# One row of small products for the scores of half a batch and one folding

## The chip, the cores and the metric

The kernel runs on one core of one Trainium2 chip. The metric is the device time of one execution in microseconds (us). Before the change the median of three runs is 1428.58 us (1428.11 to 1428.69).

## The reference, cut to what matters

Eight batches of attention over 32 memory slots are followed by two gated layers. Only the attention and the first layer bear on the change.

```python
B, H, S, D, M = 8, 8, 576, 64, 32
a = softmax(phi, axis=2)                       # pooling weights, over the 32 slots
k_m = einsum('bhsm,bhsd->bhmd', a, k)          # pooling of the keys
v_m = einsum('bhsm,bhsd->bhmd', a, v)          # pooling of the values
scores = q @ k_m.T / sqrt(D)
x = softmax(scores) @ v_m                      # all heads side by side: 4608 x 512
g = x @ w_gate;  val = x @ w_val               # 512 -> 1536
y = (silu(g) * val) @ w_out                    # 1536 -> 512
# a second layer follows: 512 -> 2048, elu, -> 512
```

## The kernel before, in words

**Folding.** The pooled values are never multiplied with the softmax. They are multiplied into the weights first: for each batch `b` and each pair `p` of 128-wide units, `vw` (line 253) forms `v_m` times a block of `w_gate` and `w_val`. This is called a folding here. Eight heads give eight small products with 64 contraction rows and 32 output columns each, 512 wide; each is two instructions in the trace, so that a folding is a row of 16. They are written to the double bank `pvw`. ScalarE then copies the high part to the tile `VW[b, p]` (line 265) and VectorE writes the low part (line 266); only then is `pvw` free. The tiles `VW` come from the pool `vx` (line 50), which has four buffers: two foldings for each of two batches.

**Scores.** `score(hf)` (line 425) does the scores of half a batch (288 positions), again with eight small products of 64 rows and 32 columns, 288 wide, 16 instructions, into the double bank `ps_sc` (line 445). VectorE then transposes both banks (450), takes a maximum (456) and subtracts it (457), and ScalarE takes the exponential (458). `norm` and `attn` follow as tasks of their own.

**Pooling.** `kv_mm` (line 384) is a row of 80 instructions for one batch, and `kv_out` copies its result with ScalarE (404). Pooling and foldings share the single double bank of the pool `ps_kv` (line 68, called `G2` from line 521 on), so each must wait until the one before it is copied out.

**The order.** The loop over `b` (from line 593 on) does batch `b`'s gates and values (`gate1`, `val1`, lines 281 to 283) for two halves of four units, and the steps `down1` (286 to 288), which are long rows of full 128x128 products. Into this main stream `tick()` (line 637) feeds a list `todo` of small tasks: the back tasks of batch `b + 1` (`back_tasks`, line 512: scores, norm, attention of the first half, then of the second), the front tasks of batch `b + 2` (`front_tasks`, line 496: three tasks of transposes `a_T`, the pooling, `kv_T`; the first batch has another list) and, at the end, the two foldings of batch `b + 1`. Front and back tasks alternate (line 631). A scheduler then fixes each engine's order: it simulates the engines and may place small tasks well ahead of the main stream if their inputs and banks are free. `together` (line 95) keeps a row's products behind its first one and lets nothing in between.

Of the kernel before, what the change touches and what calls it, by code (L numbers as in the profile page):

```python
# [8 lines left out]
F32 = mybir.dt.float32  # L9
# [29 lines left out]
def attention_moe_moe(ctx: ExitStack, tc: tile.TileContext, qT, phiT, kv, kv4, w1g, w1o, w2, out):  # L39
# [210 lines left out]

    def vw(b, p, pool=None, ps=None):
        t = VW[b, p] = vx_p.tile([128, 2, 2, 512], F32R, tag="vx", name="vw")
        both = ps or pool.tile([128, 2, 512], F32, tag="at", name="pvw")
        ps = [both[:, g] for g in range(2)]

        def head(j, g):
            r, c = slice(64 * g, 64 * g + 64), slice(32 * j, 32 * j + 32)
            return mm(ps[g][c], lhsT=Bs[b].vt[r, j, :], rhs=WG[p][j][r], start=True, stop=True)  # L260

        together([lambda j=j, g=g: head(j, g) for j in reversed(range(KD)) for g in (1, 0)])
        if b >= NEG or p >= UA // 2:
            with tc.high_priority() if pool is None else nullcontext():
                act(out=t[:, 0], in_=both, func=AF.Copy)
                tt(out=t[:, 1], in0=both, in1=t[:, 0].bitcast(F32), op=ALU.subtract)
            return
        for g in range(2):
            last["vwh"] = act(out=t[:, 0, g, :], in_=ps[g], func=AF.Copy)
        for g in range(2):  # L270
            mm(ps[g], lhsT=minus, rhs=t[:, 0, g, :], start=False, stop=True, skip_group_check=True)
            last["vwl"] = act(out=t[:, 1, g, :], in_=ps[g], func=AF.Copy)
            if g == 0:
                last["vwl0"] = last["vwl"]

# [52 lines left out]
    class Batch:  # L328
# [72 lines left out]
        def kv_out(self):  # L401
            self.kvm = fr_p.tile([128, 2, 2, D], F32, tag="kvm", name="kvm")
            for g in range(2):
                act(out=self.kvm[:, :, g, :], in_=self.kvp[g], func=AF.Copy, scale=self.rs[:, g:g + 1])


        def kv_T(self):
# [14 lines left out]

        def score(self, hf):
            q = self.qr.pop(hf)
            t = ps_at.tile([128, 2, T], F32, tag="at", name="ps_sc")
            ps = [t[:, g, :HS] for g in range(2)]
            if self.b == 0 and hf == 1:
                sc = t.rearrange("p a c -> p (a c)")  # L430
                full = sc[:, :512].rearrange("p (t g j m) -> p t j g m", t=2, g=2, j=4)
                rhs = [self.kTd[:, j].rearrange("p g m -> p (g m)") for j in range(4)]
                calls = [lambda i=i, j=j: mm(full[:, i, j], lhsT=q[:, j, 128 * i:128 * i + 128], rhs=rhs[j],
                                             start=True, stop=True) for i in range(2) for j in range(4)]
                calls += [lambda j=j: mm(t[32 * j:32 * j + 32, 1, :2 * M], lhsT=q[:, j, 256:], rhs=rhs[j],
                                         start=True, stop=True) for j in range(4)]
                together(calls)
                self.sc = bk_p.tile([128, 2, HS], F32, tag="sc", name="sc", bufs=2)
                with tc.issue_after(last["sum"].ins):
                    self.soft(self.sc, sc[:, :2 * HS].rearrange("p (b m) -> p b m", m=M))  # L440
                return

            def head(j, g):
                r = slice(64 * g, 64 * g + 64)
                return mm(ps[g][32 * j:32 * j + 32], lhsT=self.kT[r, j, :], rhs=q[r, j, :], start=True, stop=True)

            together([lambda j=j, g=g: head(j, g) for j in range(4) for g in (1, 0)])
            t = self.sc = bk_p.tile([128, 2, HS], F32, tag="sc", name="sc", bufs=2)
            for g in range(2):
                nc.vector.transpose(out=t[:, g], in_=ps[g])  # L450
            self.soft(t, t.rearrange("p g (b m) -> p (g b) m", m=M))

        def soft(self, t, x):
            sc = t.rearrange("p g (b m) -> p (g b) m", m=M)
# [56 lines left out]

    def back_tasks(b):
        z, nxt = Bs[b], Bs[b + 1] if 0 < b < B - 1 else None
        yield lambda: z.score(0)
        yield lambda: (z.norm(0), nxt and nxt.load_q(0))
        yield lambda: (z.attn(0))
        yield lambda: (z.score(1), 1 < b < B - 2 and Bs[b + 2].phi())
        yield lambda: (z.norm(1), nxt and nxt.load_q(1))
        yield lambda: (z.attn(1), z.store_at())

# [2 lines left out]
    def vw_tasks(b):  # L523
        for p in range(UA // 2):
            yield lambda p=p: vw(b, p, G2)
# [67 lines left out]
    for b in range(B):  # L593
# [30 lines left out]
            fr += [lambda: vw(0, 2, G2)] + [lambda f=f: (store_w2(), f()) for f in sets("first", 1)] + [store_w2]  # L624
            fr += [lambda: vw(0, 3, G2), lambda: load_wg(4, 1, wa_p), lambda: load_wg(5, 0, wa_p)]
        if b == 0:
            v = list(vw_tasks(1))
            todo += [bk[0], bk[1], v[0], lambda: Bs[2].phi(), bk[2], bk[3], bk[4], v[1], fr[0], fr[1], bk[5]] + fr[2:] + [lambda: Bs[3].phi()]
        else:
            for i in range(max(len(bk), len(fr))):  # L630
                todo += fr[i:i + 1] + bk[i:i + 1]
            if b + 1 < B:
                todo += vw_tasks(b + 1)
        done = [0, 0]
        spread = 18 if b == 0 else 16 if b < B - 2 else 24

# [519 lines left out]
```

## Time and profile before

| | |
|---|---|
| median of the runs | 1428.58 us |
| the profiled execution | 1427.93 us, its span 1426.2 us |
| TensorE (PE) busy | 1401.3 us, 98% of the span |
| VectorE (DVE) busy | 1136.1 us, 80% |
| ScalarE (ACT) busy | 862.4 us, 60% |
| TensorE's granted clock | 0.995 of full, over the span |

The busy time of an engine counts instructions that overlap once. PE products are pipelined: one begins while the one before is still under way, so what a product costs is the distance from its start to the next start, and not its duration. The part that the change touches lies between about 50 and 250 us.

### The profile page before, as it was taken

The numbers are of one execution on the slowest core, as the hardware profiler recorded it, in microseconds if no ns is written. First come the engines' busy times: TensorE is split into PE (matmuls) and PEld (weight loads), VectorE is DVE, ScalarE is ACT, GpSimd is POOL, SyncE is SP. The second block draws the span as 40 slices with busy tenths as digits, with TensorE's granted clock in tenths as the row PEclk, the third lists the DMA queues.
The fourth block names the chain that finished last, engine by engine and source line by source line (L and its number), as shares of the span: only waits on it lengthen the run. The fifth ranks groups of instructions, "written<-read, shape, count | busy, mean of one in ns | idle before, by whom it ended". The sixth has DMA issues, their size and how long they took to land.

```text
span 1426.2 us, 23205 instructions
## 1 busy us (share of the span) xinstructions
PE 1401.3 (98%) x9259; PEld 1211.6 (85%) x9259; DVE 1136.1 (80%) x1452; ACT 862.4 (60%) x1254; POOL 44.8 (3%) x73
## 2 busy tenths in 40 slices
PE   6899999999999999999999999999999999999998
PEld 4787889988999999999988888888888888888887
DVE  7988978778798877877988578885889488957884
ACT  5665545544465555555666388557866587548843
POOL 0000000000000000000000000000000000000000
PEclk8999999999999999999999999999999999999999
DMA  9888512664789887888889756766686667566653
GB/s 378 326 298 292 208 72 101 230 233 175 237 251 309 284 240 232 274 241 287 267 291 364 269 188 206 280 214 189 201 282 219 190 202 265 215 210 203 213 201 132
DMA packets 89484, 337.65 MB, mean 237 GB/s; under 512 B 9376, under 2 KB 23712, under 8 KB 70048
## 3 DMA queue, kind: packets, MB, share of 16 engines
q1 hardware_dynamic: 55312, 254.04, 51.6%
q10 hardware_dynamic: 26880, 51.39, 9.8%
q0 software_dynamic: 7184, 30.74, 8.9%
q8 instruction: 73, 1.20, 0.3%
q14 instruction: 35, 0.29, 0.1%
HBM read 251.13 MB, written 85.00 MB: 236 GB/s over the span
## 4 chain that ended last, share of the span: by engine, by line
PE 93%; DVE 3%; ACT 2%; DMA 1%; issue 1%; ACTq 0%; SPq 0%; DVEq 0%
PE pu L877 12%; PE pu L879 12%; PE pu L878 12%; PE pd L877 5%; PE pd L879 5%; PE pd L878 5%; PE acc L288 4%; PE acc L286 4%; PE acc L287 4%; PE pv L281 3%; PE pg L281 3%; PE pv L283 3%; PE pv L282 3%; PE pg L283 3%; PE pg L282 3%; PE pvw L260 3%
## 5 line engine op out<-in xcount | busy, mean ns | idle before, releaser
L878 PE MATMUL pu<-xlo,w 128*128 128x512 f32 x672 | 261.4, 389 | 0.0
L877 PE MATMUL pu<-xhi,w 128*128 128x512 f32 x672 | 261.4, 389 | 0.0
L879 PE MATMUL pu<-xhi,w 128*128 128x512 f32 x672 | 261.4, 389 | 0.0
L906 ACT ACTIVATE xhi<-g 128x1024 fp32r<-128x1024 f32 x120 | 126.5, 1058 | 106.9 <-PE pu L879 64.3
L907 DVE TENSOR_TENSOR xlo<-g,xhi 128x1024 fp32r<-128x1024 f32 x120 | 145.0, 1220 | 40.7 <-ACT xhi L906 40.6
L879 PEld LDWEIGHTS pu<-xhi,w 128*128 128x128 f32 x672 | 126.1, 188 | 26.3
L878 PEld LDWEIGHTS pu<-xlo,w 128*128 128x128 f32 x672 | 126.1, 188 | 26.2
L877 PEld LDWEIGHTS pu<-xhi,w 128*128 128x128 f32 x672 | 126.1, 188 | 26.1
L287 PE MATMUL acc<-hh,ws 128*128 128x288 f32 x448 | 131.7, 296 | 0.0
L286 PE MATMUL acc<-hh,ws 128*128 128x288 f32 x448 | 131.5, 295 | 0.0
L288 PE MATMUL acc<-hl,ws 128*128 128x288 f32 x448 | 128.8, 297 | 0.0
L281 PE MATMUL pv<-at,vw 128*128 128x288 f32 x384 | 115.6, 301 | 2.4 <-DVE s L306 0.7
L281 PE MATMUL pg<-at,vw 128*128 128x288 f32 x384 | 116.7, 304 | 1.1 <-ACT p L579 0.5
L767 ACT ACTIVATE hh<-gh 128x576 fp32r<-128x576 f32 x112 | 76.0, 685 | 68.6 <-PE acc L287 50.8
L282 PE MATMUL pg<-at,vw 128*128 128x288 f32 x384 | 114.1, 297 | 0.9 <-DVE at L488 0.9
L283 PE MATMUL pg<-at,vw 128*128 128x288 f32 x384 | 113.6, 296 | 0.0
L282 PE MATMUL pv<-at,vw 128*128 128x288 f32 x384 | 113.6, 296 | 0.0
L283 PE MATMUL pv<-at,vw 128*128 128x288 f32 x384 | 113.5, 296 | 0.0
L877 PE MATMUL pd<-xhi,w 128*128 128x512 f32 x288 | 112.0, 389 | 0.0
L878 PE MATMUL pd<-xlo,w 128*128 128x512 f32 x288 | 112.0, 389 | 0.0
L879 PE MATMUL pd<-xhi,w 128*128 128x512 f32 x288 | 112.0, 389 | 0.0
L897 DVE SCALAR_TENSOR_TENSOR et<-et 128x1024 f32<-128x1024 f32 x72 | 87.8, 1219 | 28.8 <-ACT et L896 28.8
(161 smaller groups left out, 3226.9 us busy)
## 6 DMA issues: line engine op xcount, KB each, us to landing
w<-dnd SPq DMA_DIRECT2D x64, 1024.0 KB, 4.9
w<-upd SPq DMA_DIRECT2D x40, 1024.0 KB, 5.7
w<-upd SPq DMA_DIRECT2D x32, 768.0 KB, 4.6
ws<-d1d SPq DMA_DIRECT2D x42, 512.0 KB, 4.5
kvr<-kv SPq DMA_DIRECT2D x32, 512.0 KB, 7.5
wr<-w SPq DMA_DIRECT2D x16, 1024.0 KB, 6.3
upd<-uw ACTq DMA_DIRECT2D x32, 512.0 KB, 6.3
dnd<-uw ACTq DMA_DIRECT2D x32, 512.0 KB, 7.9
```

The source lines that it names most:

```text
L281: mm(ps, lhsT=wh, rhs=ah, start=g == 0, stop=False)
L282: mm(ps, lhsT=wh, rhs=al, start=False, stop=False)
L283: last["pe"] = mm(ps, lhsT=wl, rhs=ah, start=False, stop=g == 1)
L286: mm(ps, lhsT=w[0][:, ms], rhs=hs[0], start=start, stop=False, skip_group_check=skip)
L287: mm(ps, lhsT=w[1][:, ms], rhs=hs[0], start=False, stop=False, skip_group_check=skip)
L288: mm(ps, lhsT=w[0][:, ms], rhs=hs[1], start=False, stop=stop, skip_group_check=skip)
L877: mm(ps, lhsT=w[0], rhs=x[0], start=start, stop=False, skip_group_check=skip)
L878: mm(ps, lhsT=w[0], rhs=x[1], start=False, stop=False, skip_group_check=skip)
L879: last["mm"] = mm(ps, lhsT=w[1], rhs=x[0], start=False, stop=stop, skip_group_check=skip)
L897: stt(out=a, in0=e, scalar=1.0, in1=a, op0=ALU.add, op1=ALU.mult)
L906: last["hi"] = act(out=hi, in_=x, func=AF.Copy)
L907: last["lo"] = tt(out=lo, in0=x, in1=hi.bitcast(F32), op=ALU.subtract)
```

## The change

From the second batch on, `score` takes the number of a folding as well: the eight products of that folding of the same batch and the eight of the scores are given to `together` as one list, foldings first. The first half's scores take folding 0, the second half's folding 1. The copies of the folding (`vw_out`) come behind the scores' softmax in program order. The separate folding tasks at the end of `todo` go, and there is a new order for loops with six front tasks, in which the pooling comes behind the second half's scores.

```diff
-    def vw(b, p, pool=None, ps=None):
-        t = VW[b, p] = vx_p.tile([128, 2, 2, 512], F32R, tag="vx", name="vw")
-        both = ps or pool.tile([128, 2, 512], F32, tag="at", name="pvw")
+    def vw_calls(b, p, ps):
         def head(j, g):
             r, c = slice(64 * g, 64 * g + 64), slice(32 * j, 32 * j + 32)
...
-        together([lambda j=j, g=g: head(j, g) for j in reversed(range(KD)) for g in (1, 0)])
+        return [lambda j=j, g=g: head(j, g) for j in reversed(range(KD)) for g in (1, 0)]
+
+    def vw(b, p, pool=None, ps=None):
+        both = ps or pool.tile([128, 2, 512], F32, tag="at", name="pvw")
+        together(vw_calls(b, p, both))
+        vw_out(b, p, both, pool)
+
+    def vw_out(b, p, both, pool=None):
+        t = VW[b, p] = vx_p.tile([128, 2, 2, 512], F32R, tag="vx", name="vw")
...
-    def score(self, hf):
+    def score(self, hf, p=None):
...
-            together([lambda j=j, g=g: head(j, g) for j in range(4) for g in (1, 0)])
+            more = p is not None and G2.tile([128, 2, 512], F32, tag="at", name="pvw")
+            with tc.issue_after(last["g2"].ins) if more else nullcontext():
+                together((vw_calls(self.b, p, more) if more else []) +
+                         [lambda j=j, g=g: head(j, g) for j in range(4) for g in (1, 0)])
             t = self.sc = bk_p.tile([128, 2, HS], F32, tag="sc", name="sc", bufs=2)
             for g in range(2):
                 nc.vector.transpose(out=t[:, g], in_=ps[g])
             self.soft(t, t.rearrange("p g (b m) -> p (g b) m", m=M))
+            if more:
+                vw_out(self.b, p, more, G2)
...
-        yield lambda: z.score(0)
+        yield lambda: z.score(0, 0 if b else None)
...
-        yield lambda: (z.score(1), 1 < b < B - 2 and Bs[b + 2].phi())
+        yield lambda: (z.score(1, 1 if b else None), 1 < b < B - 2 and Bs[b + 2].phi())
...
         if b == 0:
-            v = list(vw_tasks(1))
-            todo += [bk[0], bk[1], v[0], lambda: Bs[2].phi(), bk[2], bk[3], bk[4], v[1], fr[0], fr[1], bk[5]] + fr[2:] + [lambda: Bs[3].phi()]
+            todo += bk[:2] + [lambda: Bs[2].phi()] + bk[2:5] + fr[:2] + bk[5:] + fr[2:] + [lambda: Bs[3].phi()]
+        elif len(fr) == 6 and b < B - 2:
+            todo += [fr[0], bk[0], fr[1], bk[1], fr[2], bk[2], bk[3], fr[3], bk[4], fr[4], bk[5], fr[5]] + bk[6:]
         else:
             for i in range(max(len(bk), len(fr))):
                 todo += fr[i:i + 1] + bk[i:i + 1]
-            if b + 1 < B:
-                todo += vw_tasks(b + 1)
```

`last["g2"]` is set in `kv_out` and `vw_out`, to the instruction that last empties the shared double bank; `issue_after` orders instructions of one engine only, those of the engine that the named instruction runs on.

## Rows read from the trace of the kernel before

**Rows 1.** The page: busy time by engine, and the chain that ended last.
```profile
PE 1401.3 (98%) x9259; PEld 1211.6 (85%) x9259; DVE 1136.1 (80%) x1452; ACT 862.4 (60%) x1254; POOL 44.8 (3%) x73
PE 93%; DVE 3%; ACT 2%; DMA 1%; issue 1%; ACTq 0%; SPq 0%; DVEq 0%
```

**Rows 2.** Busy time by stretch: stretch, its length, engines' busy us (instructions), clock, DMA.
```profile
50.00:69.94 19.94, 18.98 (x284) 14.92 (x275) 19.82 (x36) 11.64 (x27) 0.00 (x0) 1.00 0.93 345
50.00:250.00 200.00, 197.75 (x2145) 169.65 (x2137) 174.64 (x332) 111.95 (x252) 0.00 (x0) 1.00 0.59 211
```

**Rows 3.** PE's waits, 50 to 250 us: for whom, us in total, times, longest.
```profile
PE pd L286 <- ACT p L579: 1.1, 2, 0.9
PE ps_kvT L410 <- ACT kvm L404: 0.5, 1, 0.5
PE pv L281 <- DVE h L313: 0.4, 1, 0.4
PE pg L281 <- DVE s L306: 0.2, 1, 0.2
```

**Rows 4.** The tiles of foldings and scores, 50 to 245 us: counts, durations, first and last start.
```profile
L260 PE MATMUL pvw<-wg,vt x224: 589/589/615, 55.4 to 238.1; 64*32 64x512 f32 x112
L445 PE MATMUL ps_sc<-qr,kT x224: 402/415/428, 54.9 to 197.2; 64*32 64x288 f32 x112
```

**Rows 5.** PE in order of time: a row of scores alone. Start us, duration us.
```profile
168.95 0.29 PE L288 MATMUL pd<-hl,woh 128*128 128x288 f32 x1
169.17 0.72 PE L445 MATMUL ps_sc<-qr,kT 64*32 64x288 f32 x16
169.82 0.40 PE L281 MATMUL pg<-at,vw 128*128 128x288 f32 x1
170.06 0.30 PE L282 MATMUL pg<-at,vw 128*128 128x288 f32 x1
170.19 0.29 PE L283 MATMUL pg<-at,vw 128*128 128x288 f32 x1
```

**Rows 6.** PE in order of time: a folding alone.
```profile
210.29 0.29 PE L288 MATMUL pd<-hl,woh 128*128 128x288 f32 x1
210.52 1.09 PE L260 MATMUL pvw<-wg,vt 64*32 64x512 f32 x16
211.54 0.40 PE L281 MATMUL pg<-at,vw 128*128 128x288 f32 x1
211.78 0.30 PE L282 MATMUL pg<-at,vw 128*128 128x288 f32 x1
```

**Rows 7.** PE in order of time: scores and a folding that already stand side by side.
```profile
96.44 0.72 PE L445 MATMUL ps_sc<-qr,kT 64*32 64x288 f32 x16
96.95 1.06 PE L260 MATMUL pvw<-wg,vt 64*32 64x512 f32 x16
97.95 0.40 PE L281 MATMUL pg<-at,vw 128*128 128x288 f32 x1
98.19 0.29 PE L282 MATMUL pg<-at,vw 128*128 128x288 f32 x1
```

**Rows 8.** PE in order of time: scores with transposes behind them.
```profile
76.35 0.29 PE L287 MATMUL pd<-hh,wol 128*128 128x288 f32 x1
76.57 0.72 PE L445 MATMUL ps_sc<-qr,kT 64*32 64x288 f32 x16
77.22 0.66 PE L380 MATMUL ps_aT<-ident,ph 128*128 128x128 f32 x4
77.63 0.38 PE L288 MATMUL pd<-hl,woh 128*128 128x288 f32 x1
77.85 0.29 PE L281 MATMUL pg<-at,vw 128*128 128x288 f32 x1
```

**Rows 9.** A folding's row on PE (batch 5) and the copy of it on ACT.
```profile
166.37 1.09 PE L260 MATMUL pvw<-wg,vt 64*32 64x512 f32 x16
171.72 1.03 ACT L265 ACTIVATE vw<-pvw 128x1024 fp32r<-128x1024 f32 x1 [0.39 <-PE pv L283]
```

**Rows 10.** DVE in order of time behind the first scores and folding of batch 1.
```profile
56.75 0.84 DVE L450 STREAM_TRANSPOSE sc<-ps_sc 128x288 f32<-128x288 f32 x2
57.62 0.75 DVE L456 TENSOR_REDUCE mx<-sc 128x18 f32<-128x576 f32 x1
58.41 0.76 DVE L457 TENSOR_TENSOR sc<-sc,mx 128x576 f32<-128x576 f32 x1
59.09 1.22 DVE L266 TENSOR_TENSOR vw<-pvw,vw 128x1024 fp32r<-128x1024 f32 x1
```

More of the change, by code (lines that the diff above doesn't have):

```diff
@@ L249, in attention_moe_moe @@
     raw = {}
-    def vw(b, p, pool=None, ps=None):
-        t = VW[b, p] = vx_p.tile([128, 2, 2, 512], F32R, tag="vx", name="vw")
-        both = ps or pool.tile([128, 2, 512], F32, tag="at", name="pvw")
-        ps = [both[:, g] for g in range(2)]
+    def vw_calls(b, p, ps):
         def head(j, g):
             r, c = slice(64 * g, 64 * g + 64), slice(32 * j, 32 * j + 32)
-            return mm(ps[g][c], lhsT=Bs[b].vt[r, j, :], rhs=WG[p][j][r], start=True, stop=True)
-        together([lambda j=j, g=g: head(j, g) for j in reversed(range(KD)) for g in (1, 0)])
+            return mm(ps[:, g][c], lhsT=Bs[b].vt[r, j, :], rhs=WG[p][j][r], start=True, stop=True)
+        return [lambda j=j, g=g: head(j, g) for j in reversed(range(KD)) for g in (1, 0)]
[5 more added lines that the diff above has]
+        t = VW[b, p] = vx_p.tile([128, 2, 2, 512], F32R, tag="vx", name="vw")
+        ps = [both[:, g] for g in range(2)]
         if b >= NEG or p >= UA // 2:
@@ L265, in vw @@
                 act(out=t[:, 0], in_=both, func=AF.Copy)
-                tt(out=t[:, 1], in0=both, in1=t[:, 0].bitcast(F32), op=ALU.subtract)
+                last["g2"] = tt(out=t[:, 1], in0=both, in1=t[:, 0].bitcast(F32), op=ALU.subtract)
             return
@@ L271, in vw @@
             mm(ps[g], lhsT=minus, rhs=t[:, 0, g, :], start=False, stop=True, skip_group_check=True)
-            last["vwl"] = act(out=t[:, 1, g, :], in_=ps[g], func=AF.Copy)
+            last["vwl"] = last["g2"] = act(out=t[:, 1, g, :], in_=ps[g], func=AF.Copy)
             if g == 0:
@@ L403, in kv_out @@
             for g in range(2):
-                act(out=self.kvm[:, :, g, :], in_=self.kvp[g], func=AF.Copy, scale=self.rs[:, g:g + 1])
+                last["g2"] = act(out=self.kvm[:, :, g, :], in_=self.kvp[g], func=AF.Copy, scale=self.rs[:, g:g + 1])
         def kv_T(self):
```

## The prediction

> **What bounds the kernel now.** I read the page first, then the busy time by stretch, then TensorE's waits, and last TensorE's instructions in order of time. The page says that TensorE is busy for 98% of the span and that 93% of the chain that ended last runs through it [rows 1]. The change touches only the stretch from 50 to 250 us, and there the picture is the same: 197.75 of 200 us busy at the full granted clock [rows 2]. The missing 2.2 us are explained by five waits, the longest 0.9 us [rows 3]. So a microsecond taken out of TensorE's queue here is a microsecond off the end, as long as no new wait takes its place. VectorE is the engine to watch: 174.64 of 200 us, and in the first 20 us of the stretch 19.82 of 19.94 [rows 2].
>
> How much a row of small products costs must be read from starts, since durations overlap. In the main stream one full product starts 0.13 us after the other (170.06 to 170.19) [rows 5].
>
> **What the change removes.** *A row of scores alone* [rows 5]: the row starts 0.22 us after the product ahead of it, the next full product 0.65 us after the row's start, and the one after that 0.24 us later. That is 1.11 us for what would be two steps of 0.13 without the row: the row costs 0.85 us. *A folding alone* [rows 6]: 0.23, 1.02 and 0.24 us, 1.49 less 0.26: 1.23 us. Apart they cost 2.08 us.
>
> *The two side by side* already occur [rows 7]: the folding starts 0.51 us after the scores' start, where a full product starts after 0.65. So 0.14 us of the 0.65 is the change from small products to full ones, and is not paid between small ones. Then 1.00 us to the first full product and 0.24 to the second. With an entry of 0.22 that is 1.97 less 0.26, or 1.71 us. The new row has the folding first. No row shows that order; by the same 0.14 the folding takes 1.02 - 0.14 = 0.88 and the scores behind it 0.65, in all 0.22 + 0.88 + 0.65 + 0.24 - 0.26 = 1.73 us. A joined pair therefore saves 2.08 - 1.73 = 0.35 us: one entry (0.09 above the normal step), one change (0.14) and one late second product (0.11). The nearest rows bound it between 0.34 (those three terms) and 0.37 (2.08 - 1.71).
>
> *How many pairs.* Batches 1 to 7 have 14 rows of scores and 14 foldings (224 instructions each, 16 to a row) [rows 4]. I followed all 28 through TensorE's order: twice a folding already stands directly behind scores, as at 96.44 [rows 7] and once at 54.93. The other 12 pairs stand apart: 12 x 0.35 = 4.2 us. Some rows have transposes as neighbours instead of full products. That doesn't change the count: scores with transposes behind them take 0.22 + 0.65 to the transposes, and four transposes and the way back 0.41 + 0.22 [rows 8], so the row itself pays the same entry and exit.
>
> **What it moves.** Each folding's copy (1.03 us on ScalarE, 1.22 us on VectorE) and each softmax stay, in number and size. They lie beside TensorE's work; I cost them at nothing, and the cover is the 25 us in which VectorE is free [rows 2]. No DMA is added; the loads and stores issued by the same tasks (q, phi, the store of the attention) move with them, and SP's queue is passed by no one.
>
> The new order for six front tasks is, as I read the code, never taken. From the third batch on `front_tasks` yields five (three transposes, pooling, `kv_T`); the loops that could take the branch have five. They keep the alternating list, with the pooling ahead of the second half's scores. So the last part of the title does not happen, and something near its opposite does: pooling and foldings share one double bank, and a bank is handed on in program order. Before, the second half's scores needed nothing of that bank. Now their row must wait for the pooling's copy-out, and the first half's row for the copy of the folding before.
>
> *The wait behind the copies.* A copy of a folding waits in turn for its `VW` buffer: batch 5's folding ran at 166.37, its copy at 171.72, when batch 3's last product had read the buffer [rows 9]. So scores can no longer run ahead of the foldings. Their last start moves from 197 toward 238 us [rows 4]. Is anything then late? The second half's scores of a batch stand with its second folding, whose buffer comes free at the end of the batch two before; between that and their first use lie a whole batch and half of the next, twelve units of 24 full products, 12 x 24 x 0.13 = 37 us at least. The softmax begins with 2.4 us of VectorE [rows 10] and has a few steps more. It is not late.
>
> What can cost is TensorE standing at the head of such a row when the simulated copy ends sooner than the real one: the whole main stream is queued behind it. `issue_after` orders only instructions of the engine that it names, ScalarE or VectorE, so it does not hold these products back. Five rows (second halves of batches 2 to 6) get the new wait on the pooling's copy. The nearest row is the same copy making `kv_T` wait once in seven, 0.51 us [rows 3]. From both sides: at best all waits of the stretch vanish with the new order, -2.2 us; at worst each of the five rows waits as long as the longest wait, 5 x 0.9 = +4.5 us [rows 3]. I take one wait of 0.51 us, the nearest row's rate.
>
> **The sum.** -4.2 + 0.5 = -3.7 us. The profiled execution took 1427.93 us (span 1426.2 and 1.7 around it); it would take 1424.2. It lies 0.65 below the median of the runs, so I forecast a median of 1424.9 us. With the bounds of the wait: 1422.2 (-4.2 - 2.2) to 1428.9 (-4.2 + 4.5).
>
> **The rivals.** A measurement of this kernel tells 0.2%, about 2.9 us, from no change.
>
> 1. *The new waits eat the gain.* All five rows stand 0.51 us behind the pooling's copy: -4.2 + 2.6 = -1.6, 1427.0 us. For it: `kv_T` hangs on the same copy and did wait. Against: it waited once in seven, and 2.2 us is all that TensorE waits in 200 us.
>
> 2. *Slower: VectorE gets its work in lumps.* A joined row hands VectorE 0.84 + 0.75 + 0.76 us of softmax and 1.22 us of folding at once, 3.6 us [rows 10], where before these came mostly apart. Gates and values need VectorE to free their three banks, and a unit of 24 products lasts 3.1 us; if the lump is placed ahead of their steps, TensorE stops. Its price is that of the longest wait, 0.9 us per row, and it decides from the fifth row on (4.2 / 0.9 = 4.7); at ten of 14 rows it is 9.0 - 4.2 = +4.8, 1433.4 us. For it: VectorE is full in the first 20 us. Against: at 96.44 and 54.93 the lump already exists, and TensorE's waits on VectorE sum to 0.6 us [rows 3]. The Trainium skill, TensorEngine Tiling (Array Packing), section PSUM Bottleneck, speaks for this rival: packing small products speeds TensorE up but not the emptying of its banks, which may become the bound. The trace so far bears that out only in part.
>
> 3. *The rows don't join.* If the scheduler did not keep the 32 products together, or put the pairs back apart, the time stays at 1428.6 us. For it: scores and folding have different inputs. Against: `together` has kept every row of 16 whole.
>
> 4. *Better than forecast.* The order also loses the old waits: 1422.2 us.
>
> **How the numbers follow.** Forecast 0.53, rival 1 0.20, rival 2 0.14, rival 3 0.08, rival 4 0.05. Forecast and rival 4 are faster by over 0.2%: 0.58. Rivals 1 and 3 lie within it, with a small part of rival 2: 0.29. The rest of rival 2 is slower: 0.13. The forecast's own range is 1422.2 to 1425.7. For 8 in 10 I add rivals 1 and 3 and the lower part of rival 2 above, and a little below for the scheduler's luck: 1421.8 to 1430.8 us.
>
> **What would show it.** Right: 14 rows of 32 small products between 50 and 250 us, the score products starting about 0.88 us after the row's start and the first full product about 1.5; the last scores start near 238 instead of 197; every row of a second half of batches 2 to 6 comes behind a pooling row; the stretch up to the last unit of batch 7 is shorter by 3 to 5 us, and everything after is only shifted. Wrong: waits of TensorE on a copy of pooling or folding at several rows (rival 1), more than 4 us of waits on VectorE's steps of gates and values (rival 2), or fewer than 14 joined rows (rival 3). The forecast fails as a whole if TensorE's idle time in the stretch grows by more than the 4.2 us that its queue loses.

## The result: slower, 1436.57 us

The changed kernel takes 1436.57 us (median of six runs, 1434.9 to 1438.74) against 1428.34 us for the kernel before in the same series; the ratio is 1.0059, with a 95% interval of 1.0046 to 1.0072. The forecast was 1424.9 us, and no more than 1430.8: the direction was wrong. In the order of the prediction's views, the page of the profile after (answering to [rows 1]) has its span, the busy times and the shares of the chain that ended last:

```profile
span 1437.0 us, 23205 instructions
PE 1401.1 (98%) x9259; PEld 1213.6 (84%) x9259; DVE 1137.0 (79%) x1452; ACT 862.2 (60%) x1254; POOL 44.9 (3%) x73
PE 84%; DVE 8%; DMA 4%; ACT 2%; issue 2%; ACTq 0%; SPq 0%; DVEq 0%
```

The work is the same to the instruction. What has changed is the chain: TensorE's share falls from 93 to 84%, VectorE's rises from 3 to 8%, that of transfers from 1 to 4%. The end is now held up by others for a while. The longer transfers in it are those of `phi` (at 46.6, 106.8 and 163.2 us) and, new, of the weights `w1o` and `w1g` (at 239.6, 286.7, 310.1 and 333.6 us). Where TensorE lost the time is read from the busy time by stretch (columns as in [rows 2]):

```profile
50.00:250.00 200.00, 190.87 (x2098) 166.75 (x2087) 166.58 (x317) 107.99 (x244) 0.00 (x0) 1.00 0.59 209
250.00:300.00 50.00, 46.86 (x370) 43.11 (x369) 38.63 (x67) 26.01 (x54) 0.00 (x0) 1.00 0.51 178
```

TensorE stands idle for 9.13 of the 200 us, where it was 2.25 [rows 2], and for 3.14 of the next 50 us, where before it was 0.47 (50 less 49.53 busy). From 300 to 400 us the same view gives 3.08 against 1.42. That is 11.2 us of added idle time, and the clock is at full speed in both kernels. Behind 400 us nothing changes: the first product of the second layer starts at 735.3 instead of 724.5, 10.8 us late, and the spans differ by 10.8 us too.

Who is waited for, 50 to 300 us (answering to [rows 3]):

```profile
PE pv L287 <- DVE s L312: 3.0, 3, 1.6
PE pg L287 <- ACT p L590: 2.4, 4, 0.9
PE pg L287 <- DVE s L312: 2.2, 2, 1.4
PE pvw L257 <- DVE smx L475: 1.3, 1, 1.3
PE ps_kvm L403 <- DVE vw L272: 1.3, 1, 1.3
PE pvw L257 <- DVE vw L272: 0.6, 2, 0.5
PE pd L292 <- ACT woh L195: 0.4, 1, 0.4
PE pg L288 <- DVE at L499: 0.2, 1, 0.2
PE ps_aT L386 <- ACT vt L427: 0.2, 1, 0.2
```

Most of it (7.6 us) is for the main stream's own helper steps: the gate step `s` on VectorE (line 312, 306 before) and the copy `p` on ScalarE (590, 579 before), whose ends free the three banks that gates, values and the downward products share. What the prediction feared, the shared bank of pooling and foldings, is the smaller part (lines 475 and 272: 3.2 us; the step of line 475 is a small one of the norm that ran right behind line 272's copy, which had emptied the bank).

The joined rows themselves are as forecast. One in TensorE's order of time (start us, duration us):

```profile
97.61 1.09 PE L257 MATMUL pvw<-wg,vt 64*32 64x512 f32 x16
98.49 0.69 PE L451 MATMUL ps_sc<-qr,kT 64*32 64x288 f32 x16
99.11 0.40 PE L287 MATMUL pg<-at,vw 128*128 128x288 f32 x1
99.35 0.30 PE L288 MATMUL pg<-at,vw 128*128 128x288 f32 x1
```

The scores start 0.88 us after the row's start and the first full product 1.50 us after it, and the next 0.24 us later: to the digit or nearly so. There are 14 such rows, and the last scores start at 243.7 (forecast: near 238). The tiles' view, to be held against [rows 4]:

```profile
L257 PE MATMUL pvw<-wg,vt x224: 589/601/613, 55.3 to 243.0; 64*32 64x512 f32 x112
L451 PE MATMUL ps_sc<-qr,kT x224: 402/402/403, 56.2 to 243.7; 64*32 64x288 f32 x112
```

To see both sides at once I cut TensorE's order of time, from 27 us to the second layer's first product, into steps from one start to the next and added them up by kind. Steps that end in a named wait go from 14.5 us (15 steps) to 28.8 us (28 steps), +14.3; all other steps from 683.6 to 680.0, -3.7: together 10.7 of the 10.8 us. The 13 steps that came into the first group took their normal length with them, so neither number is a price by itself. Less the normal step at each place, the waits are 9.6 us before and 22.2 us after (27 to 400 us): +12.6 us. That leaves 1.8 us by which everything else became shorter.

**What such a wait looks like.** At 125.54 TensorE has four transposes, and then stands still until 127.52:

```profile
125.54 0.60 PE L386 MATMUL ps_aT<-ident,ph 128*128 128x128 f32 x4
127.52 0.40 PE L287 MATMUL pg<-at,vw 128*128 128x288 f32 x1 [1.38 <-DVE s L312]
```

ScalarE's half of the gate step that it needs was done at 124.10 (the instruction of line 311 starts at 123.71 and takes 0.39 us). VectorE's queue in that time:

```profile
123.84 0.75 DVE L474 TENSOR_REDUCE smx<-sc 128x18 f32<-128x576 f32 x1
124.63 0.18 DVE L475 TENSOR_SCALAR smx<-smx 128x18 f32<-128x18 f32 x1
124.84 0.27 DVE L476 RECIPROCAL smx<-smx 128x18 f32<-128x18 f32 x1
125.02 0.42 DVE L459 STREAM_TRANSPOSE sc<-ps_sc 128x288 f32<-128x288 f32 x1
125.37 0.71 DVE L477 TENSOR_TENSOR sc<-sc,smx 128x576 f32<-128x576 f32 x1
126.00 0.47 DVE L459 STREAM_TRANSPOSE sc<-ps_sc 128x288 f32<-128x288 f32 x1
126.39 0.73 DVE L496 STREAM_TRANSPOSE ex<-sc 128x576 f32<-128x576 f32 x1
127.05 0.42 DVE L312 SCALAR_TENSOR_TENSOR s<-s,pg 128x288 f32<-128x288 f32 x1
```

VectorE is never idle here, and the gate step, ready since 124.10, starts 2.95 us later, behind seven small steps. Norm of one half, transposes of the next scores and the transpose for the attention stand in a row: a lump.

Not every wait is a lump. Between 250 and 300 us there are no joined rows at all, and there the longest wait, 1.65 us at 270.35, comes from ScalarE's queue:

```profile
266.31 0.37 ACTq L204 DMA_DIRECT2D d1d<-uw  x1
266.72 0.45 ACT L298 ACTIVATE hh<-h 128x288 fp32r<-128x288 f32 x1 [0.45 <-DVE h L319]
266.80 1.24 ACTq L591 DMA_DIRECT2D p1d<-p  x1
268.08 1.28 ACTq L204 DMA_DIRECT2D d1d<-uw  x1
269.40 0.71 ACT L311 ACTIVATE s<-pg 128x288 f32<-128x288 f32 x2 [2.23 <-PE pd L294]
```

Two issues of stores took 1.24 and 1.28 us, where the one ahead of them took 0.37. ScalarE's half of two gate steps stood behind them. Single slow issues are not new: the kernel before has two between 27 and 400 us, 0.85 us at 291.3 and 1.52 at 341.6.

### The profile page after: what moved, and what is told of

It is laid out like the page before. It is cut to its first block, busy times and chain, and to the rows that moved or that the text cites. A ratio compares the mean times of both kernels' runs of the same rounds, so it can differ in the third digit from the quotient of the medians.

```text
span 1437.0 us, 23205 instructions
## 1 busy us (share of the span) xinstructions
PE 1401.1 (98%) x9259; PEld 1213.6 (84%) x9259; DVE 1137.0 (79%) x1452; ACT 862.2 (60%) x1254; POOL 44.9 (3%) x73
## 4 chain that ended last, share of the span: by engine, by line
PE 84%; DVE 8%; DMA 4%; ACT 2%; issue 2%; ACTq 0%; SPq 0%; DVEq 0%
PE pu L889 12%; PE pu L887 12%; PE pu L888 12%; PE pd L889 5%; PE pd L887 5%; PE pd L888 5%; PE acc L294 4%; PE acc L292 4%; PE acc L293 4%; PE pg L287 3%; PE pv L287 3%; PE pv L289 3%; PE pv L288 3%; PE pg L288 3%; PE pg L289 3%; PE pvw L257 2%
## 5 line engine op out<-in xcount | busy, mean ns | idle before, releaser
L907 DVE SCALAR_TENSOR_TENSOR et<-et 128x1024 f32<-128x1024 f32 x72 | 87.9, 1221 | 28.8 <-ACT et L906 28.8
```

Of the source, the lines that this page charges most:

```text
L907: stt(out=a, in0=e, scalar=1.0, in1=a, op0=ALU.add, op1=ALU.mult)
```

## The experiments

The theories on trial: the joined row makes lumps on VectorE (rival 2); the shared bank of foldings and pooling makes TensorE wait; small work now comes too late; the loops have two tasks fewer, so that `tick()` feeds the rest at another pace; the second buffer of `phi` is missing; VectorE as a whole is too full for any order but a lucky one. Ratios are to the kernel before in the same series, with 95% intervals. "Waits" are the sum just described, one profiled execution each, to be held against 9.6 us of the kernel before and 22.2 of the changed one. The kernel before took 1426.9 to 1428.3 us as the median of its series, so where medians of two series are subtracted below, a difference under some 2 us says little, and the intervals decide.

**1. Which part of the change is it?** *apart* keeps both moves but not the joining:

```diff
-        yield lambda: z.score(0, 0 if b else None)
+        yield lambda: z.score(0)
...
+        if bk:
+            for i, p in ((3, 1), (0, 0)):
+                bk[i] = lambda p=p, b=b, f=bk[i]: (f(), vw(b + 1, p, G2))
```

> The foldings stay where the change put them (beside the scores of the same half, ahead of and behind the pooling), but as rows of their own: scores are no longer bound to the shared double bank and nothing is joined. Theory A (the move: bank and copies now interleave with the pooling and tie the small tasks together): the loss stays and the joins' 4.2 us come on top, 1438 to 1441 us. Theory A1 (only the binding of the scores to the bank costs): 1428 to 1431. Theory B (the joined row hands VectorE one lump): the lumps are gone, 1428 to 1432.

1438.15 us, ratio 1.0072 (1.0057 to 1.0087), waits 18.6 us. Without a single joined row the loss is there in full; the medians differ by 1.6 us, which the intervals don't separate, and the profiled spans are 1436.8 us here and 1437.0 us in the changed kernel. Joining does take time out: outside the waits the changed kernel needs 3.4 us less (1437.0 less 22.2, against 1436.8 less 18.6). But as much, 3.6 us, comes back as waits; from 50 to 250 us TensorE is idle for 6.1 us in *apart* and for 9.1 us in the changed kernel. The lumps of joined rows cannot be the main cause.

*first_only* joins the first half's row only and leaves the other folding at the end of the list, as a task:

```diff
-        yield lambda: (z.score(1, 1 if b else None), ...
+        yield lambda: (z.score(1), ...
...
+            if b + 1 < B:
+                todo += [lambda b=b: vw(b + 1, 1, G2)]
```

> Only the first half's scores are joined with folding 0; the second half's scores stand alone and folding 1 is again the last task of the loop. Seven joins save 2.4 us. Theory A and A1: the second half's scores no longer wait for the pooling's and the folding's copies, at least half of the loss goes: 1427 to 1432. Theory B: seven lumps of fourteen are left, half of the loss: 1431 to 1433. If the time is below 1427 the second half's row alone carried the loss.

1436.76 us, ratio 1.0062 (1.0048 to 1.0075), waits 16.2 us. Half the joins, the same loss: it doesn't go by the number of joined rows.

*copy_first* puts the folding's copies ahead of the scores' transposes and softmax:

```diff
+            if more:
+                vw_out(self.b, p, more, G2)
             t = self.sc = bk_p.tile(...)
...
             self.soft(t, t.rearrange("p g (b m) -> p (g b) m", m=M))
-            if more:
-                vw_out(self.b, p, more, G2)
```

> As the changed kernel, but the folding's copies come ahead of the softmax in program order, so that the shared bank is free about 2.4 us earlier and the softmax later. Theory A (the waits on the bank): the 3.3 us of waits on the folding's copies go, 1432 to 1434. Theory B: the lump is the same size, within 1.5 us of the changed kernel, 1435 to 1438.

1435.97 us, ratio 1.0059 (1.0045 to 1.0072), waits 19.6 us. The place of the copies is worth 0.6 us, which the runs don't tell from nothing.

*pool_behind* makes the dead branch live, for the five front tasks that there are, so that the new order, with the pooling behind the second half's scores, does take place:

```diff
-        elif len(fr) == 6 and b < B - 2:
-            todo += [... bk[3], fr[3], bk[4], fr[4], bk[5], fr[5]] + bk[6:]
+        elif len(fr) == 5 and b < B - 2:
+            todo += [... bk[3], fr[3], bk[4], fr[4], bk[5]] + bk[6:]
```

> The branch that was never taken, made to be taken with five front tasks: the pooling behind the second half's scores, as the title has it. Theory A: the second row no longer waits for the pooling's copy-out, but the pooling waits for both foldings' copies, which wait for their buffers: the sign is open, 1430 to 1440. Theory B: the same lumps, 1434 to 1439. If the title's order is what the change needs, it is below 1428.

1434.21 us, ratio 1.0046 (1.0033 to 1.0059), waits 19.1 us. The pooling's place gives back at most 2.4 us of the 8.2 (1436.57 less 1434.21), and the intervals of the two ratios overlap; the loss stays.

**2. Is it lateness or the shared bank?** *held* is the kernel before, with the pooling and the scores on TensorE kept from starting before a unit of the main stream, about where the changed kernel has them; *held_pool* holds the pooling alone.

```diff
+    def held_to(key):
+        return tc.issue_after(unit_mm[key].ins) if key in unit_mm else nullcontext()
...
-            together([... pooling ...])
+            together([... pooling ...], (self.b - 3, 1, 1))
...
-            together([... scores ...])
+            together([... scores ...], (self.b - 3, 1, 3) if hf == 0 else (self.b - 2, 1, 1))
```

> The kernel before, with its foldings, banks and task list untouched; only TensorE may not take the small rows as far ahead of the main stream as before: the pooling of a batch not before unit 2 of the second half three batches earlier, its first half's scores not before the end of that batch, its second half's scores not before unit 2 of the second half two batches earlier, which is about where the changed kernel has them (last pooling at 211 instead of 186 us, last scores at 242 instead of 197). Theory L (the loss is lateness: in the changed kernel the pooling stands behind a folding's copy, which waits for its buffer, so pooling, scores and softmax come up to a batch later and crowd VectorE beside the weight conversions of batches 6 and 7): 1434 to 1440 us. Theory W (the loss is the waits on the shared bank and the folding's new neighbours themselves): 1427 to 1430. Theory R (any reordering away from the old schedule costs): 1431 to 1438.

> As held, but only the pooling is held back; the scores may run ahead as far as their own inputs allow. Theory L: the scores of the next batch hang on the pooling, so most of the loss comes with it: 1432 to 1438. Theory W: 1427 to 1430. Theory R: 1431 to 1438.

*held*: 1431.02 us, ratio 1.0023 (1.0014 to 1.0032), waits 11.4. *held_pool*: 1432.5 us, 1.0028 (1.0019 to 1.0038), waits 14.2. Holding the small work back costs some 3 to 5 us where the change cost 8.2, so that lateness could explain about half at most. Holding more costs no more than holding less.

The next two move the pooling of batches 2 to 7 into the scores' double bank, once in *apart*, once in the kernel before:

```diff
-                t = ps_kv.tile([128, 2, 512], F32, tag="at", name="ps_kvm")
+                t = (ps_at if self.b > 1 else ps_kv).tile([128, 2, 512], F32, tag="at", name="ps_kvm")
```

> The kernel with the foldings beside their scores but not joined (1438.2 us), and the pooling from the third batch on in the scores' double bank instead of the foldings': the pooling is behind scores, which are emptied at once, and no longer behind a folding's copy. Theory L: pooling and scores run ahead again, 1427 to 1431. Theory W: 1434 to 1439, since the foldings still stand at the new place with the same copies. Theory R: 1431 to 1438.

> The kernel before with the same move of the pooling into the scores' double bank: its foldings and pooling no longer wait for each other. Theory L: the small work can run further ahead still, 1424 to 1428.5. Theory W: fewer waits on the bank, but there were hardly any, 1427 to 1429. Theory R: 1431 to 1438.

*apart_pool_bank*: 1434.61 us, ratio 1.0046 (1.0032 to 1.006), waits 16.6. *before_pool_bank*: 1431.77 us, 1.0025 (1.0016 to 1.0034), waits 12.2. With the pooling out of the foldings' bank *apart* gains 3.5 us and keeps 6.8. Given the same, the kernel before gets slower by 4.0 us. The bank is a part at most.

**3. Is it the pace?** *padded* is the changed kernel with two empty tasks per loop, so that its lists are as long as before. *before_unpadded* is the opposite control: the kernel before with its two foldings run inside the last task, so that they join nothing and little but the list's length changes.

```diff
+            if b + 1 < B:
+                todo += 2 * [lambda: None]
```
```diff
-            if b + 1 < B:
-                todo += vw_tasks(b + 1)
+            if b + 1 < B:
+                todo[-1] = lambda f=todo[-1], b=b: (f(), vw(b + 1, 0, G2), vw(b + 1, 1, G2))
```

> As the changed kernel, with two empty tasks in each loop's list at the places where the foldings' tasks were. Rows, joins and banks are as in the changed kernel; only the pace is the old one again: with two tasks fewer, the weights of batches 2 to 5 (the last real task of the list) and the weight sets of the last loops are handed in later, and each following weight fetch waits for the one raw buffer. Theory P (the pace carries a large part of the loss, above all the 2.7 us at 250 to 275 that every kernel with moved foldings shows): 1428 to 1433.5 us. Theory W (waits on the shared bank) and theory L (lateness of pooling and scores): 1435 to 1438.

> The kernel before, with its two foldings run inside the last task of the list instead of as two tasks behind it: nothing is joined and the foldings' order in the bank is the old one, but the list is as short as in the changed kernel. Theory P: slower by 3 us or more, 1431 to 1437, with idle time of TensorE at 250 to 275. Theories W and L: 1427 to 1430.

*padded*: 1441.81 us, ratio 1.0098 (1.0084 to 1.0112), waits 26.1. *before_unpadded*: 1438.42 us, 1.0079 (1.0065 to 1.0092), waits 17.1. The control loses 11 us, more than the whole change, without a joined row and with the last scores at 204.8 us, not far from the 197.2 of the kernel before [rows 4]. Its waits, 50 to 300 us, and the busy time of a stretch:

```profile
PE pg L281 <- DVE s L306: 4.1, 3, 2.1
PE pd L286 <- DVE h L313: 2.5, 1, 2.5
PE ps_kvT L410 <- ACT kvm L404: 1.8, 1, 1.8
PE pd L286 <- ACT woh L195: 0.4, 1, 0.4
PE pd L286 <- ACT p L579: 0.2, 1, 0.2
```
```profile
250.00:300.00 50.00, 47.48 (x363) 44.72 (x369) 36.70 (x63) 25.52 (x54) 0.00 (x0) 0.97 0.54 182
```

Again the gate and value steps (306 and 313). The granted clock is part of this loss: right behind the waits of 2.07 us (ended at 145.82) and 2.52 us (ended at 264.94) it is at the lower of its two levels (1.2 instead of 2.4 GHz) for a while, 0.97 over the last stretch, and full products start 0.24 us apart (146.23 to 146.47) instead of 0.13. Of the 10.1 us by which the profiled span is longer (1436.3 against 1426.2), the waits are 7.5 (17.1 less 9.6); the rest is mostly this. In *held*, *pool_behind_padded* and *ph2* the clock falls in the same way, in the kernel before and the changed one never between 50 and 400 us. But the pace is not the cause in the simple sense either, since the old pace made the changed kernel worse. Two more bear on it; both add the empty tasks to a kernel shown above.

> The title's order (pooling behind the second half's scores) with the two empty tasks. Without them it took 1434.2. Theory P: 1426 to 1431. Theories W and L: 1433 to 1436.

> Only folding 0 joined, folding 1 at the end as before, one empty task in the place of folding 0. Without it, 1436.8. Theory P: 1427 to 1431. Theories W and L: 1435 to 1438.

*pool_behind_padded*: 1440.51 us, ratio 1.0092 (1.0078 to 1.0105), waits 22.7; *first_only_padded*: 1434.49 us, 1.0055 (1.0041 to 1.0069), waits 16.1. The padding costs 6.3 us in one; in the other the median is 2.3 us lower, which the intervals don't separate. The old pace helps clearly in none of the three. One wait does follow the pace: 2.5 us for the value step at 263 to 265 us stands in *before_unpadded* and in *first_only*, but not in the kernel before and not in *first_only_padded* (0.2 us).

**4. Is VectorE too full?** *light* leaves the norm's four VectorE steps (sum, a small addition, reciprocal, product: 0.75 + 0.18 + 0.27 + 0.71 = 1.9 us) out of batches 2 to 7, 23 us in all, so its softmax is not normed there. *before_light* and *apart_light* leave out the same.

```diff
+            if self.b > 1:
+                return
             sm = bk_p.tile([128, 2 * HS // M, 1], F32, tag="smx", name="smx", bufs=2)
             nc.vector.tensor_reduce(out=sm, in_=sc, op=ALU.add, axis=AX.X)
```

> The changed kernel without the four steps that normalise the softmax (sum, add, reciprocal, product) for batches 2 to 7: 12 x 1.9 = 23 us less for VectorE between 75 and 270 us, nothing less for TensorE; compare it with before_light. Theory V (the joins do save 4.2 us of TensorE, and the loss is gate and value steps that stand in VectorE's and ScalarE's fixed queues behind small work): with VectorE eased at least half of the 8 us difference goes, 1426 to 1431. Theory S (the waits come from the order of rows, banks and transfers, whatever VectorE's load): 1433 to 1437.

> The kernel before without the same four steps for batches 2 to 7, as the measure for light. Theory V and theory S: VectorE was off the path here, 1424 to 1428; what counts is light minus before_light (V: under 4 us, below zero if the joins' saving comes through; S: 7 to 9 us). Theory R (any other order than the old one costs, even with less work): 1430 or more.

> The kernel with the foldings beside their scores but not joined, again without the four normalising steps for batches 2 to 7. Without that easing it took 1438.2 against 1436.6 joined. Theory V: its loss goes too, and what is left over light (1427.25) is the joins' saving alone, 3 to 5 us: 1430 to 1433. Theory S, or if the one eased kernel was luck: 1435 or more. If it is at 1427 as well, the joins save nothing that reaches the end.

*light*: 1427.25 us, ratio 1.0000 (0.9992 to 1.0009), waits 11.5. *before_light*: 1428.47 us, 1.0008 (0.9999 to 1.0017), waits 10.4. *apart_light*: 1434.2 us, 1.0049 (1.0036 to 1.0062), waits 15.7. With this work left out the change costs nothing: 1427.25 against 1428.47, a difference that the intervals don't separate. The waits of *light*, 50 to 300 us, and its busy time:

```profile
PE pg L287 <- DVE s L312: 1.7, 3, 0.8
PE pd L292 <- DVE h L319: 1.4, 2, 1.2
PE pg L287 <- ACT p L592: 0.9, 1, 0.9
PE pvw L257 <- ACT vt L427: 0.2, 1, 0.2
```
```profile
50.00:250.00 200.00, 195.98 (x2162) 172.75 (x2155) 159.15 (x286) 113.08 (x253) 0.00 (x0) 1.00 0.60 213
```

Idle time of TensorE in the stretch is 4.0 us instead of 9.1, and 0.25 us instead of 3.1 from 250 to 300 us. *apart_light* speaks against a full explanation. It gets only 4.0 us faster than *apart* (1438.15 less 1434.2), and waits still stand at the gate and value steps. Three of its five lines from 50 to 300 us:

```profile
PE pd L292 <- DVE h L319: 2.8, 1, 2.8
PE pg L287 <- DVE s L312: 2.5, 3, 1.3
PE pvw L257 <- ACT kvm L410: 1.7, 2, 0.9
```

*pool_norm* takes work from VectorE without leaving any out: the norm's product goes to GpSimd from batch 2 on.

```diff
-            tt(out=sc, in0=sc, in1=sm.to_broadcast([128, 2 * HS // M, M]), op=ALU.mult)
+            (nc.gpsimd.tensor_tensor if self.b > 1 else tt)(out=sc, in0=sc, in1=..., op=ALU.mult)
```

> The changed kernel, complete, with the product of the normalisation (0.75 us on VectorE, 12 times) done by GpSimd, which is idle 97% of the time. Theory V: VectorE has 9 us less between 75 and 270 us, a third to a half of the loss goes: 1428 to 1434; under 1427 it beats both kernels. Theory S: 1435 to 1438. Should GpSimd be slow, the attention comes later by its longer product, which has a batch of slack.

1436.62 us, ratio 1.007 (1.0056 to 1.0084), waits 19.6: no gain. Its busy time shows how small the relief was (the fifth pair of numbers is GpSimd), and two lines in order of time show why:

```profile
50.00:250.00 200.00, 192.83 (x2110) 168.30 (x2101) 165.37 (x309) 109.60 (x247) 13.82 (x11) 1.00 0.59 209
```
```profile
154.72 1.16 POOL L477 TENSOR_TENSOR sc<-sc,smx 128x576 f32<-128x576 f32 x1 [20.26 <-DVE smx L476]
155.15 1.04 DVE L300 TENSOR_TENSOR hl<-h,hh 128x288 fp32r<-128x288 f32 x1 [0.57 <-ACT hh L298]
```

The 11 products take 13.82 us there, 1.26 each against 0.71 on VectorE, so about 8 us leave VectorE (11 x 0.71) and each norm's chain grows by half a microsecond. But much of it comes back: VectorE's step of line 300, 0.45 us as a rule, took 1.04 us where it began during GpSimd's product. Seven steps of the lines 300 and 132 met one in this way and took 5.1 us longer in all, and over the whole span VectorE's busy time falls only from 1137.0 to 1134.0 us. So this run did not ease VectorE much and says little about its load.

**5. Who is served first?** *prio* gives the steps that free the main stream's banks (gate, value, split, the copy `p`) a higher priority on ScalarE and VectorE. *ph2* gives `phi` a second buffer, because VectorE once stood 2.34 us behind its transfer (in the kernel before the longest such wait is 2.16 us).

```diff
-            last["s"] = act(out=s, in_=pg, func=AF.Tanh, scale=0.5)
-            stt(out=s, in0=s, scalar=1.0, in1=pg, op0=ALU.add, op1=ALU.mult)
+            with tc.high_priority():
+                last["s"] = act(out=s, in_=pg, func=AF.Tanh, scale=0.5)
+                stt(out=s, in0=s, scalar=1.0, in1=pg, op0=ALU.add, op1=ALU.mult)
```
```diff
-            self.ph = fr_p.tile([128, 2, S], F32, tag="ph", name="ph")
+            self.ph = fr_p.tile([128, 2, S], F32, tag="ph", name="ph", bufs=2)
```

> The changed kernel with the gates' and values' steps on ScalarE and VectorE, and the copies of the downward products, at high priority in the scheduler; TensorE's rows stay in the same order up to batch 7. Theory V: these steps no longer stand behind small work where the scheduler has the choice, 1428 to 1433. Theory S: 1435 to 1438.

> The changed kernel with a second buffer for phi, so that its transfer starts earlier: VectorE stood 4.2 us in four waits for it (2.3 us at 112.7), with gate steps behind. If these waits carry the loss: 3 to 5 us less, 1431 to 1434. If not: 1435 to 1438.

*prio*: 1434.27 us, ratio 1.0049 (1.0035 to 1.0062), waits 18.7. The median is 2.3 us lower, though the intervals overlap, and most of that is seen from 250 to 300 us, where the idle time falls from 3.1 to 1.4 us. *ph2*: 1442.7 us, 1.0111 (1.0097 to 1.0125), waits 25.5: worse by 6 us. The waits for the transfer only got shorter, 2.9 us in two instead of 4.2 in four, and the order had more waits elsewhere: the first joined row comes at 61.3 us instead of 55.3, behind TensorE's waits of 2.1 and 1.6 us (ended at 47.2 and 50.7) with a granted clock of 0.73 from 50 to 60 us. So the late transfer is neither shown nor excluded as a part of the loss.

No kernel that does the whole computation beat the one before. *light* equals it, with 23 us of work left out.

## Why the prediction was wrong

**The saving came, but smaller.** Fourteen joined rows, 0.88 us to the scores and 0.62 from there to the full product, second-half rows behind the pooling, the dead branch: these steps held. The forecast was 4.2 us out of TensorE's queue. Outside the named waits the changed kernel needs 1.8 us less than the kernel before, and 3.4 us less than *apart*; *light* needs 3.0 us less than *before_light* (spans less waits: 1413.7 and 1416.7). The term that was too large is the late second product, 0.11 us a pair, 1.3 us in all. The plain steps from one full product to the next, 4290 before with 585.4 us and 4286 after with 586.0 us, have become 1.1 us longer (0.6, and 4 x 0.13 for the four that are fewer) instead of 1.3 us shorter. These 2.4 us are all that is missing: the other steps are together 2.9 us shorter, where entry and change were to give 12 x 0.23 = 2.8. From 50 to 250 us the late second products behind small rows and transposes fall only from 41 to 34, not by 12, since behind transposes, which now stand alone more often, they rise from 14 to 18. What the prediction says of rows beside transposes, "That doesn't change the count", was therefore not right. And behind a named wait the second product is late as well (127.52 to 127.76 is 0.24 us instead of 0.13), 19 times instead of 12. What else made these steps longer I can't place.

**That the softmax would not be late** held nearly. With the last scores at 243.7 instead of 197.2 us, waits for the attention's last step on VectorE (line 499, 488 before) rose from 1.1 to 1.6 us.

**The step that failed** is that of the copies and the softmax: "They lie beside TensorE's work; I cost them at nothing, and the cover is the 25 us in which VectorE is free", and the wait of 0.51 us that was all I put against it, with a bound of +4.5 us. Measured were +12.6 us of named waits (22.2 less 9.6). The 25 us were a sum over 200 us. They say nothing about whether VectorE is free in the microsecond in which a gate step becomes ready, and where a step has to wait for all that stand ahead of it in the engine's fixed order, that is what counts: at 124.10 VectorE was not free, for 2.95 us.

The added waits by what was waited for, after against before, 27 to 400 us: VectorE's gate step 6.7 against 1.2 us, ScalarE's copy `p` 4.3 against 2.8, the shared bank's emptying on VectorE (lines 272 and 475; 266 before) 4.4 against 0.4. These three are 11.0 of the 12.6 us. So in the profiled executions the sum is 12.6 - 1.8 = +10.8 us, where it was to be 0.5 - 4.2 = -3.7; the medians lie 8.2 us apart, since the profiled execution of the changed kernel was the longest of its six runs (1438.74) and that of the kernel before (1427.93) lay below its median.

**The bounds were too narrow for the same reason.** The worst case was "each of the five rows waits as long as the longest wait", so only rows with a new dependency could wait. More than half of the new waits (7.0 of 12.6 us, for `s` and `p`) are at products whose dependencies are unchanged. They depend on the order in which the scheduler's simulation laid out VectorE and ScalarE, and that order is new for the whole attention part; the added idle time reaches up to 400 us, far behind the last joined row.

**Rival 2** came nearest: VectorE as the place, the gate and value steps as those that wait, 1433.4 us as the time, and a chance of 0.14. Its mechanism, a price per joined row, is refuted as the main cause: *apart*, without joined rows, loses 10.6 us, and *before_unpadded* 11.1. The part of the waits that goes with joining is the 3.6 us from *apart* (18.6) to the changed kernel (22.2), about what joining took out of the queue. The Trainium skill, TensorEngine Tiling (Array Packing), section PSUM Bottleneck, spoke for rival 2: packing speeds TensorE up but not the emptying of its banks, which may become the bound. The trace agrees only in part: most of the new waits are for steps that empty banks, on a VectorE that was 87% busy in the stretch before [rows 2], but *apart*, which joins nothing, has 9.0 of the 12.6 us as well. **Rival 1** had its place, waits at the shared bank, but that is the smaller part, and with the pooling moved to the scores' bank *apart* was still 6.8 us slow.

**What is shown and what stays open.** Shown: the time is lost in waits of TensorE, more than half of them on helper steps of the main stream; joining does not cause the most of them; not one change of a single suspect (bank, pace, place of the copies or of the pooling, `phi`) removes more than half of the loss, and lateness put into the kernel before makes about half of it at most; leaving 23 us of VectorE's steps out removes it all in the changed kernel. And the order before is hard to beat: all 16 kernels that do the whole computation with its small work in another order or place are slower by 3 to 16 us. Twelve of them contain the change's own moves, so they are no fair sample; the four that start from the kernel before and join nothing lose 3 to 11 us. Open: which of the displaced steps costs which wait, what the later transfers of the weights `w1o` and `w1g` contribute (the first `w1o` at 239.5 instead of 230.3 us), which no run tried by itself, why *apart* keeps more than half of its loss with VectorE eased, and whether leaving the norm out helps by its load or by being one more change of the order. I would not put the loss down to one mechanism. With such differences between orders, a saving of 4 us could only have shown if the order had stayed as good.

## What to carry to other kernels

Where one engine is busy for 98% and a helper for 87%, each working through a fixed order, moved helper work is not free because the helper has time in sum: look at what stands in the queue when a step of the main stream becomes ready, and set the bound of the cost from the whole stretch, not from the rows with new dependencies. Before believing a mechanism, run a control that only disturbs the order (here *before_unpadded*, +11 us): it tells the scatter against which a saving of 0.3% must be seen. Whether easing the helpers first would win such a saving is not shown: *light* did not clearly beat *before_light*.

## What the runs showed of the hardware

- Issues of transfers on ScalarE's queue took 0.33 us in the median (82 in the changed kernel from 27 to 400 us), but the two at 266.80 and 268.08 took 1.24 and 1.28 us, and two later ones 1.65 and 1.43. The gate steps queued behind the first two started at 269.40, where their last products had started at 268.01. The kernel before has two such issues as well (0.85 and 1.52 us). What makes them slow was not tried.
- The norm's product took 1.26 us on GpSimd on average (13.82 us for 11; most took 1.16, the longest 1.96) against 0.71 on VectorE for the same 128x576 operands.
- While GpSimd's product ran, VectorE's steps with two operands in SBUF got longer: line 300 took 0.73 to 1.42 us instead of 0.45 (five times) and line 132 took 2.16 instead of 1.22 (twice). Line 319, with one of its two tensors in a bank of TensorE, took the usual 0.45 us.
- TensorE's granted clock fell to its lower level right behind waits of 2.07 and 2.52 us in *before_unpadded*. It did not behind one of 2.59 us (ended at 264.94) in *apart*. So a long wait can cost more than its length, and does not always.
